# Sparse attention and soft mixture of experts on one core: the factor on the keys moves from the key tile to the instruction that negates the scores

## The chip, the cores and the metric

One Trainium2 chip, one of its cores. The metric is the device time of one execution in microseconds (us); the kernel before was run three times: 547.24, 548.01 and 548.21 us, median 548.01 us. The engines are called PE (TensorE; PEld is its weight load), DVE (VectorE), ACT (ScalarE), POOL (GpSimd) and SP (SyncE, which here issues the DMAs).

## The reference

Attention over 8 batches and 8 heads, 576 tokens, head size 64, in fp32. Scores that lie more than `tau` below their row's maximum are dropped, and the output of attention feeds a soft mixture of experts (8 experts with 4 slots each, hidden size 1024).

```
scores = scale * q @ k.T                     # scale = 1/8
thresh = max(scores, -1) - tau
scores = where(scores >= thresh, scores, -1e9)
attn   = exp(scores - max(scores, -1));  attn /= sum(attn, -1) + 1e-9
x      = (attn @ v), heads side by side      # 4608 x 512
logits = x @ phi                             # 4608 x 32
slots  = softmax(logits, over tokens).T @ x; out_e = relu(slots_e @ w1_e) @ w2_e
out    = softmax(logits, over slots) @ out_e
```

## The kernel before, in words

The 64 heads are worked on as 32 pairs (two heads of a batch, one on the upper and one on the lower 64 partitions), four pairs to a batch. For a pair SP loads the keys into a tile `k` (128 x 576, L525), the queries into `q` (L530) and the values into `vv` (L537); `k` and `q` have two buffers each.

Before the keys are used they are multiplied by `flag8`, a column of 128 numbers that holds 1/8 (or 0 for a negative tau; L392): for the first pair by two instructions of DVE, one per half of the tile (128 x 288), for the other 31 pairs by one instruction of POOL on the whole tile (both L532).

A pair then has nine blocks of scores. For each block
- PE computes q times k into one of four PSUM regions `ps` (L552, for the ninth block L557),
- DVE reads the region once and writes the negated scores `ss` to SBUF, and on the way takes their minimum, the negated maximum, as the column `nmx` (L564; the profile names it TENSOR_SCALAR_CACHE_REDUCE, with a DVE_READ_ACCUMULATOR behind it). Here it is called the negation,
- ACT computes the exponential into `p` (L574),
- POOL adds |tau| to the column `nmx`, which gives `thr` (L577),
- DVE compares `ss` with `thr`, multiplies `p` by the result and sums the rows (L580, SCALAR_TENSOR_TENSOR). Here it is called the masking.

PE transposes `p` (L478), ACT copies the transposes out of PSUM (L483), and PE multiplies them with the values (L670). POOL and DVE form reciprocals of the row sums (L604, L607, L615, L618), which POOL applies (L611, L689). At the end of a batch come the logits (L752) and the sums of the slots (L800, L805, L813). Behind the last pair the experts' weights (`w`, `host`) are used and the output is written (L997 to L1086).

The order of all instructions up to the last pair is computed when the kernel is built: class `Order` holds each step with its engine, a duration, its dependences and a due time (`TABLE`, by the number of the step in its scope). A planner then goes through time, and gives each engine that is free the step with the earliest due time whose inputs are there and which has room in its buffers. `G.skip(n)` counts numbers without adding a step, so that the due times of the steps behind keep their places. Each engine carries out its list in this order and waits on semaphores; `qload` holds the number of the step that loads the queries of a pair, behind which two weight loads are put.

Of the kernel before, what the change touches and what calls it, by code (L numbers as in the profile page):

```python
# [10 lines left out]
F32 = mybir.dt.float32  # L11
F32R = mybir.dt.float32r
AF = mybir.ActivationFunctionType
ALU = mybir.AluOpType
# [8 lines left out]
    k=2, q=2, vv=2, r=3, ri=3, nmx=4, thr=4, p2=4, pL=1, pTa=1, pTb=1, pTl=1, l4=1,  # L23
    ss=4, xT=5, x=1, xl=1, dT=1, d=1, M=2, f=2,
# [313 lines left out]
def softmax_attention_soft_moe(  # L338
# [17 lines left out]
    nc = tc.nc  # L356
# [9 lines left out]
    HS = S // 2  # L366
# [3 lines left out]
    cp = ctx.enter_context(tc.tile_pool(name="consts", bufs=1))  # L370
# [8 lines left out]
        out=st1, in_=ident.rearrange("p (g s) -> p s g", g=4), axis=AX.X, op=ALU.add  # L379
# [8 lines left out]
    phi_sb = cp.tile([128, HP, NS], F32, name="phi_sb")  # L388
    tau_sb = cp.tile([128, 1], F32, name="tau_sb")
    nc.sync.dma_start(tau_sb, tau.to_broadcast([128, 1]))  # L390
    flag8 = cp.tile([128, 1], F32, name="flag8")
    nc.vector.tensor_scalar(  # L392
        out=flag8, in0=tau_sb, scalar1=0.0, scalar2=0.125, op0=ALU.is_ge, op1=ALU.mult
    )
    NR = 4 * B + B // 2
    lall = cp.tile([128, NR, NS], F32, name="lall")
# [18 lines left out]
    with tc.tile_pool(name="ps_up", bufs=1, space=PSUM) as up:  # L415
# [6 lines left out]
        k=([128, S], F32), q=([128, 2, S], F32), vv=([128, 640], F32), r=([128, N9], F32), ri=([128, N9], F32),  # L422
        nmx=([128, 1], F32), thr=([128, 1], F32), p2=([128, 2 * S], F32), pL=([128, S], F32),
        pTa=([128, 2, 4, QA], F32), pTb=([128, 2, 4, S - QA], F32), pTl=([128, S], F32), l4=([128, 192], F32),
        ss=([128, S], F32), xT=([128, S], F32), x=([128, 4, DM], F32), xl=([128, DM], F32), dT=([128, 192], F32),
# [5 lines left out]
    G = Order(kinds)  # L431
# [14 lines left out]
    n = NPRE + NHOST  # L446
# [44 lines left out]
    def dve(dur, nom, r, w, fn):  # L491
        G.add("DVE", dur, nom, fn, r, w)
# [11 lines left out]
    def pair(p):  # L504
        b, j = divmod(p, HP)
        t0 = p * N9
        late = p == NP - 1
        G.scope("first" if p == 0 else "last" if p == NP - 1 else f"pair{j}", t0)
        kt, qt, vv = (Buf(k) for k in ("k", "q", "vv"))
# [5 lines left out]
        def pool(dur, nom, fn, r, w):  # L515
            G.add("POOL", dur, nom, fn, r, w)


        one = dict(scalar2=1.0, op0=ALU.mult, op1=ALU.mult)
        parts = [(h,) for h in range(2)] if p == 0 else [(0, 1)]  # L520
        for hs in parts:
            kc, n = slice(hs[0] * HS, (hs[-1] + 1) * HS), len(hs)
            def keys(a=hs[0], z=hs[-1] + 1):
                for g in range(2):
                    nc.sync.dma_start(  # L525
                        kt.t[rows[g]].rearrange("p (h k) -> p h k", h=2)[:, a:z],
                        kT[b, j, :, 0:2 * S].rearrange("d (h g k) -> d g h k", h=2, g=2)[:, g, a:z])
            G.add("SP", 1340 if p else 700, t0 - 18 + hs[0], keys, w=[kt[h] for h in hs])
            for g in range(2):
                G.add("SP", (625 if p == 0 else 1250) if p < 3 else 800, t0 - 18 + hs[0], lambda g=g, a=hs[0], z=hs[-1] + 1: nc.sync.dma_start(  # L530
                    qt.t[rows[g], a:z], qT[b, j, :, a:z]), w=[qt[h, g] for h in hs])
            sc = lambda e, kc=kc: lambda: e.tensor_scalar(out=kt.t[:, kc], in0=kt.t[:, kc], scalar1=flag8, **one)  # L532
            if p == 0:
                G.add("DVE", 370, t0 - 9 + hs[0], sc(nc.vector), [], [kt[h] for h in hs])
            else:
                pool(730, t0 - 9, sc(nc.gpsimd), [], [kt[h] for h in hs])
        G.add("SP", 1400 if p < 3 else 800, t0 - 12, lambda: nc.sync.dma_start(vv.t, vt[b, j]), w=[vv], after=vload[-1:])  # L537
        vload.append(len(G.ops) - 1)
        qload.append(len(G.ops) - 2 - (p > 0))

# [1 line left out]
        for i in range(N9):  # L544
            t = t0 + i
            s, nmx, thr = Buf("s"), Buf("nmx"), Buf("thr")
            c, h = divmod(i, 2)

            def qk(i=i, c=c, h=h, s=s):
# [12 lines left out]
            ss = Buf("ss")  # L562

            dve(674, t + OFF['mx'], [s], [ss, nmx], lambda s=s, ss=ss, nmx=nmx: nc.vector.tensor_scalar(  # L564
                out=ss.t.rearrange("p (a k) -> p a k", a=2), in0=s.t[:, :, 0:HS], scalar1=-1.0, scalar2=3.4028234663852886e38,
                op0=ALU.mult, op1=ALU.min, accum_out=nmx.t))
            sv = lambda ss=ss: ss.t.rearrange("p (a k) -> p a k", a=2)
            if i == 8:
# [1 line left out]
            else:  # L570
                if h == 0:
# [6 lines left out]
                out=thr.t, in0=nmx.t, scalar1=1.0, scalar2=pabs, op0=ALU.mult, op1=ALU.add), [nmx], [thr])  # L578
            G.add("DVE", 738, t + OFF['st'], port=True, r=[ss, thr], w=[dst, r[i]],
                fn=lambda sv=sv, thr=thr, view=view, i=i: nc.vector.scalar_tensor_tensor(  # L580
                    out=view().rearrange("p (a k) -> p a k", a=2), in0=sv(),
                    scalar=thr.t, in1=view().rearrange("p (a k) -> p a k", a=2),
                    op0=ALU.is_le, op1=ALU.mult, accum_out=r.t[:, i:i + 1]))

            if late and i == 8:
                dve(70, t + OFF['ri'], [r], [ri], lambda: nc.vector.tensor_scalar(
                    out=ri.t, in0=r.t, scalar1=1e-9, scalar2=None, op0=ALU.add))
# [14 lines left out]
            elif i == 8:  # L602
                e = slice(i // 2 * 2, i + 1)
                pool(292, t + OFF['ri'], lambda e=e: nc.gpsimd.tensor_scalar(  # L604
                    out=ri.t[:, e], in0=r.t[:, e], scalar1=1e-9, scalar2=1.0, op0=ALU.add, op1=ALU.mult),
                    [r[k] for k in range(e.start, e.stop)], [ri[c]])
                dve(84, t + OFF['ri'], [], [ri[c]], lambda e=e: nc.vector.reciprocal(ri.t[:, e], ri.t[:, e]))  # L607
                for k in range(e.start, e.stop):
# [3 lines left out]
                        out=view(), in0=view(), scalar1=ri.t[:, k:k + 1], **one), [ri[c]], [dst_])  # L612
            elif not late and h == 1:
                if i == 7:
                    pool(292, t + OFF['ri'], lambda: nc.gpsimd.tensor_scalar(  # L615
                        out=ri.t[:, 0:8], in0=r.t[:, 0:8], scalar1=1e-9, scalar2=1.0, op0=ALU.add, op1=ALU.mult),
# [43 lines left out]
        for a, (pT, q) in enumerate(((pTa, slice(0, QA)), (pTb, slice(QA, S)))):  # L660
            n0 = u + OFF['a1' if a else 'a0']
            w = bank_of(p == NP - 1)
            n = q.stop - q.start
# [10 lines left out]
            if late:  # L674
                dve(69 + 1.04 * n, n0 + OFF['ae'], [w, spreads[0]], [xT[a]], lambda w=w, q=q, n=n: nc.vector.tensor_tensor(
                    out=xT.t[:, q], in0=lone(w)[:, 0:n], in1=spreads[0].t[:, q], op=ALU.mult))
# [9 lines left out]
        if not late:  # L686
# [3 lines left out]
                out=wide(), in0=wide(), in1=ri.t[:, 0:8].rearrange("p (c h) -> p c h", h=2).unsqueeze(3).to_broadcast(  # L690
                    [128, 4, 2, 64]), op=ALU.mult))
# [159 lines left out]
    recent, last, vload, qload = [], [], [], []  # L851
    for p in range(NP):
        recent.append(len(G.ops))
        pair(p)
        if p % HP == HP - 1:
            dispatch(p // HP)
# [54 lines left out]
    for i in range(NHOST):  # L911
        n = next(n for n in reversed(range(len(cells))) if sum(map(bytes_of, cells[n:])) >= (i + 1) * 4096)
# [262 lines left out]
```

## Time and profile before

| what | value |
|---|---|
| runs | 547.24, 548.01, 548.21 us; median 548.01 us |
| span of the profiled execution (first to last instruction) | 546.2 us |
| median of the runs less this span | 1.8 us |
| PE, PEld busy | 527.5 us (97%), 337.0 us (62%) |
| DVE, ACT, POOL busy | 471.0 us (86%), 457.4 us (84%), 242.1 us (44%) |
| mean granted clock of TensorE | 0.993 of full speed |

The page gives no other time for the profiled execution than its span; the 1.8 us are taken for what lies around it. Busy time is the union of an engine's instructions. A DVE instruction's row ends some 0.07 us after the start of the next one, so how long an instruction holds DVE is read from one start to the next. Ends of matmuls are modelled, so that a PE row may hide a short wait. Under "idle before" stands the idle time of the engine ahead of an instruction, and what ended it.

### The profile page before, as it was taken

The page shows a single profiled execution, that of the slowest core. Times are in us where ns is not written, and L with a number is a line of the kernel's source. Part 1 is how long each engine was busy: PE and PEld are TensorE (multiplying, and loading weights), DVE is VectorE, ACT ScalarE, POOL GpSimd, SP SyncE. Part 2 cuts the span into 40 slices and gives each one's busy share as a digit, 9 for nine tenths or more (in the row PEclk, how much of TensorE's full clock was granted, in tenths as well). Part 3 has the DMA queues.
Part 4 walks back from the last instruction along what each step waited for, and adds up shares of the span by engine and source line. Part 5 has one row for each costly group of instructions (what it writes and reads, how often), then busy time and mean ns, then how long its engine had stood idle before and what let it go on. Part 6 is the DMA issues. An engine that isn't in the chain of part 4 may idle for free.

```text
span 546.2 us, 18324 instructions
## 1 busy us (share of the span) xinstructions
PE 527.5 (97%) x7029; PEld 337.0 (62%) x7029; DVE 471.0 (86%) x1332; ACT 457.4 (84%) x790; POOL 242.1 (44%) x475
## 2 busy tenths in 40 slices
PE   8999999999999999999999999999999999999990
PEld 6666666666666666666666666666666656644470
DVE  5999998999999999999899989999999999523192
ACT  3899998999899989999999989999999888621181
POOL 2554555554545464545355545545454524121030
PEclk9999999999999999999999999999999999999997
DMA  6355555565535543333333333333333322999498
GB/s 176 74 158 178 168 167 169 138 190 161 166 90 167 172 153 122 92 94 86 78 91 92 91 91 92 91 91 91 91 90 91 91 76 69 336 410 408 197 375 316
DMA packets 31990, 83.03 MB, mean 152 GB/s; under 512 B 4640, under 2 KB 12832, under 8 KB 31904
## 3 DMA queue, kind: packets, MB, share of 16 engines
q1 hardware_dynamic: 31904, 81.87, 48.8%
q8 instruction: 55, 0.90, 0.7%
q14 instruction: 31, 0.25, 0.2%
HBM read 72.42 MB, written 9.44 MB: 150 GB/s over the span
## 4 chain that ended last, share of the span: by engine, by line
PE 82%; DVE 5%; DMA 5%; ACT 4%; issue 2%; DVEq 0%; POOL 0%; SPq 0%; POOLq 0%; ACTq 0%
PE ps L670 29%; PE ps L552 24%; PE ps L478 17%; DMA w<-in_w 5%; PE ps L557 3%; PE ps L694 2%; PE ps L752 2%; PE ps L800 1%; DVE p L580 1%; PE up L418 1%; DVE cT L989 1%; DVE host L1086 1%; ACT pTa L483 1%; DVE ss L564 1%; PE ps L470 1%
## 5 line engine op out<-in xcount | busy, mean ns | idle before, releaser
L564 DVE TENSOR_SCALAR_CACHE_REDUCE ss<-ps 128x576 f32<-128x576 f32 x288 | 209.1, 752 | 15.5 <-ACT pTl L483 4.8
L577 POOL TENSOR_SCALAR thr<-nmx,pabs 128x1 f32<-128x1 f32 x288 | 132.2, 461 | 187.0 <-DVE ss L564 167.7
L580 DVE SCALAR_TENSOR_TENSOR p<-ss,thr,p 128x576 f32<-128x576 f32 x256 | 201.8, 823 | 3.4 <-ACT p L574 3.1
L574 ACT ACTIVATE p<-ss,nmx 128x576 f32<-128x576 f32 x256 | 188.2, 781 | 18.3 <-DVE ss L564 18.2
L552 PE MATMUL ps<-k,q 64*128 64x288 f32 x1024 | 167.2, 427 | 1.0 <-ACT pTb L483 0.4
L478 PE MATMUL ps<-ident,p 64*128 64x64 f32 x2304 | 98.2, 223 | 0.9 <-ACT pTa L483 0.3
L478 PEld LDWEIGHTS ps<-ident,p 64*128 64x128 f32 x2304 | 87.8, 138 | 17.8 <-issue 3.3
L552 PEld LDWEIGHTS ps<-k,q 64*128 64x128 f32 x1024 | 83.3, 188 | 21.9 <-ACT pTl L652 5.8
L483 ACT COPY pTb<-ps 128x1024 f32<-128x1024 f32 (+1 forms) x96 | 84.0, 876 | 5.7 <-PE ps L478 3.5
L670 PE MATMUL ps<-pTb,vv 128*64 128x320 f32 x512 | 76.0, 439 | 0.4 <-DVE pTl L652 0.4
L483 ACT COPY pTa<-ps 128x1024 f32<-128x1024 f32 x64 | 64.9, 1018 | 0.4 <-PE ps L478 0.4
L670 PE MATMUL ps<-pTa,vv 128*64 128x256 f32 x512 | 62.3, 385 | 0.0
L670 PEld LDWEIGHTS ps<-pTb,vv 128*64 128x64 f32 x512 | 34.1, 136 | 36.4 <-issue 9.0
L670 PEld LDWEIGHTS ps<-pTa,vv 128*64 128x64 f32 x512 | 33.9, 136 | 26.2 <-DVE ss L564 8.5
L670 PE MATMUL ps<-pTl,vv 128*64 128x256 f32 (+1 forms) x256 | 41.9, 406 | 0.0
L689 POOL TENSOR_TENSOR x<-x,ri 128x512 f32<-128x512 f32 x31 | 32.3, 1043 | 4.8 <-ACT x L483 4.8
L483 ACT COPY xT<-ps 128x256 f32<-128x256 f32 (+1 forms) x62 | 24.6, 398 | 6.2 <-PE ps L670 5.2
L670 PEld LDWEIGHTS ps<-pTl,vv 128*64 128x64 f32 x256 | 18.5, 137 | 12.6
L580 DVE SCALAR_TENSOR_TENSOR pL<-ss,thr,pL 128x576 f32<-128x576 f32 x32 | 26.0, 812 | 0.0
L574 ACT ACTIVATE pL<-ss,nmx 128x576 f32<-128x576 f32 x32 | 24.8, 776 | 0.4 <-DVE ss L564 0.4
L954 POOL TENSOR_TENSOR c<-lall,crow 128x512 f32<-128x512 f32 x9 | 9.3, 1046 | 35.7 <-PE ct L470 21.4
L483 ACT COPY pTl<-ps 128x256 f32<-128x256 f32 x64 | 24.2, 378 | 0.4 <-PE ps L478 0.4
(165 smaller groups left out, 550.3 us busy)
## 6 DMA issues: line engine op xcount, KB each, us to landing
w<-in_w SPq DMA_DIRECT2D x44, 512.0 KB, 7.3
q<-in_qT SPq DMA_DIRECT2D x62, 288.0 KB, 4.5
vv<-in_vt SPq DMA_DIRECT2D x32, 320.0 KB, 4.6
host<-in_w SPq DMA_DIRECT2D x20, 512.0 KB, 7.8
k<-in_kT SPq DMA_DIRECT2D x62, 144.0 KB, 3.0
out<-w SPq DMA_DIRECT2D x8, 512.0 KB, 3.4
out<-host SPq DMA_DIRECT2D x8, 512.0 KB, 5.0
out<-host SPq DMA_DIRECT2D x4, 256.0 KB, 4.6
```

What stands on the lines that cost most here:

```text
L478: nc.tensor.transpose(out=s[:, g, c:c + 64], in_=ins[g], identity=ident[rows[g], rows[g]], tile_position=(64 * g, 0))
L483: G.add("ACT", 51 + 0.833 * n, nom, lambda: nc.scalar.copy(*io()), r, w)
L552: nc.tensor.matmul(s.t[:, g, 0:HS], qt.t[rows[g], h, c * 128:(c + 1) * 128], kt.t[rows[g], h * HS:(h + 1) * HS], start=True, stop=True, ti ...
L557: nc.tensor.matmul(s.t[rows[a], g, 0:HS], qt.t[rows[g], a, SM:S], kt.t[rows[g], a * HS:(a + 1) * HS], start=True, stop=True, tile_position ...
L564: dve(674, t + OFF['mx'], [s], [ss, nmx], lambda s=s, ss=ss, nmx=nmx: nc.vector.tensor_scalar(out=ss.t.rearrange("p (a k) -> p a k", a=2), ...
L574: G.add("ACT", 668, t + OFF['ex'], lambda sv=sv, nmx=nmx, view=view: nc.scalar.activation(view().rearrange("p (a k) -> p a k", a=2), sv(), ...
L577: pool(250, t + OFF['th'], lambda nmx=nmx, thr=thr: nc.gpsimd.tensor_scalar(out=thr.t, in0=nmx.t, scalar1=1.0, scalar2=pabs, op0=ALU.mult, ...
L580: fn=lambda sv=sv, thr=thr, view=view, i=i: nc.vector.scalar_tensor_tensor(out=view().rearrange("p (a k) -> p a k", a=2), in0=sv(), scalar ...
L670: nc.tensor.matmul(lone(w)[h * 64:(h + 1) * 64, 0:n], vv.t[:, v0:v0 + 64], p0, start=(kb == 0), stop=(kb == 4), tile_position=(0, h * 64), ...
L689: G.add("POOL", 1040, u + 6.8, own=f"new{j}", r=[ri[0]], w=[x[j]], fn=lambda: nc.gpsimd.tensor_tensor(out=wide(), in0=wide(), in1=ri.t[:, ...
L694: nc.tensor.transpose(out=w.t[:, g, c * 64:c * 64 + 64], in_=xj()[rows[g], c], identity=ident[rows[g], rows[g]], tile_position=(64 * g, 0))
L752: nc.tensor.matmul(lone(wl)[c * 32:(c + 1) * 32, o], phi_sb[:, k, :], xT[k].t[:, q(c)], start=(k == 0 and not o.start), stop=(k == HP - 1) ...
```

## The change

The column becomes `nflag8` = -1/8 (or 0), and the negation multiplies by that column where it multiplied by the constant -1.0. The two instructions of DVE and the 31 of POOL on the keys are left out. `G.skip(1)` stands in their place, and the number in `qload` is corrected for the step that is no longer there.

```
-    flag8 = cp.tile([128, 1], F32, name="flag8")
+    nflag8 = cp.tile([128, 1], F32, name="nflag8")
     nc.vector.tensor_scalar(
-        out=flag8, in0=tau_sb, scalar1=0.0, scalar2=0.125, op0=ALU.is_ge, op1=ALU.mult
+        out=nflag8, in0=tau_sb, scalar1=0.0, scalar2=-0.125, op0=ALU.is_ge, op1=ALU.mult
     )
...
-            sc = lambda e, kc=kc: lambda: e.tensor_scalar(out=kt.t[:, kc], in0=kt.t[:, kc], scalar1=flag8, **one)
-            if p == 0:
-                G.add("DVE", 370, t0 - 9 + hs[0], sc(nc.vector), [], [kt[h] for h in hs])
-            else:
-                pool(730, t0 - 9, sc(nc.gpsimd), [], [kt[h] for h in hs])
+            G.skip(1)
...
-        qload.append(len(G.ops) - 2 - (p > 0))
+        qload.append(len(G.ops) - 2)
...
             dve(674, t + OFF['mx'], [s], [ss, nmx], lambda s=s, ss=ss, nmx=nmx: nc.vector.tensor_scalar(
-                out=ss.t.rearrange("p (a k) -> p a k", a=2), in0=s.t[:, :, 0:HS], scalar1=-1.0, scalar2=3.4028234663852886e38,
+                out=ss.t.rearrange("p (a k) -> p a k", a=2), in0=s.t[:, :, 0:HS], scalar1=nflag8, scalar2=3.4028234663852886e38,
                 op0=ALU.mult, op1=ALU.min, accum_out=nmx.t))
```

The changed file is five lines shorter from the keys on, so that the negation is L564 before and L559 after, the scores L552 and L547, the masking L580 and L575.

On DVE at the start of the kernel (first the columns made from tau, then the first blocks of pair 0) the order before is:

```order
L392 TENSOR_SCALAR flag_78<-tau_sb 128x1
L407 TENSOR_SCALAR nabs<-tau_sb 128x1
L409 TENSOR_SCALAR pabs<-nabs 128x1
L532 TENSOR_SCALAR k_312<-k_312,flag_78 128x288 x2
L378 TENSOR_REDUCE st_66<-ident 128x32
L564 TENSOR_SCALAR ss_216,nmx_268<-ps_336 128x576
L564 TENSOR_SCALAR ss_240,nmx_256<-ps_337 128x576
```

The same place with the change:

```order
L392 TENSOR_SCALAR nflag_78<-tau_sb 128x1
L407 TENSOR_SCALAR nabs<-tau_sb 128x1
L409 TENSOR_SCALAR pabs<-nabs 128x1
L378 TENSOR_REDUCE st_66<-ident 128x32
L559 TENSOR_SCALAR ss_216,nmx_268<-ps_336,nflag_78 128x576
L559 TENSOR_SCALAR ss_240,nmx_256<-ps_337,nflag_78 128x576
```

The two instructions on `k` are gone, and the negation has the column as one more input. The rest of DVE's list stands in the same order to its end.

On POOL in the second pair (`thr` is the threshold, `ri` the reciprocals, `pL` the ninth block) the order before is:

```order
L615 TENSOR_SCALAR ri_280<-r_308 128x8
L577 TENSOR_SCALAR thr_292<-nmx_300,pabs 128x1
L532 TENSOR_SCALAR k_312<-k_312,flag_78 128x576
L577 TENSOR_SCALAR thr_248<-nmx_268,pabs 128x1
L577 TENSOR_SCALAR thr_260<-nmx_256,pabs 128x1
```

With the change:

```order
L610 TENSOR_SCALAR ri_280<-r_308 128x8
L572 TENSOR_SCALAR thr_292<-nmx_300,pabs 128x1
L572 TENSOR_SCALAR thr_248<-nmx_268,pabs 128x1
L572 TENSOR_SCALAR thr_260<-nmx_256,pabs 128x1
```

One instruction of 128 x 576 per pair is gone from between the thresholds, and nothing else is moved. PE, ACT and SP have the same instructions in the same order as before; of the PSUM regions two change their places at a few steps.

## Rows read from the trace of the kernel before

**Rows 1.** The page: busy time of the engines, and the clock granted to TensorE in 40 slices.

```profile
PE 527.5 (97%) x7029; PEld 337.0 (62%) x7029; DVE 471.0 (86%) x1332; ACT 457.4 (84%) x790; POOL 242.1 (44%) x475
PEclk9999999999999999999999999999999999999997
```

**Rows 2.** Busy time in four stretches: the first pairs, the middle, the last pairs, the experts. Columns: us, then PE, PEld, DVE, ACT, POOL busy (instructions), granted clock, DMA share, GB/s.

```profile
20.00:47.80 27.80, 27.00 (x328) 16.71 (x326) 27.18 (x78) 25.07 (x42) 15.42 (x29) 1.00 0.53 142
47.80:434.00 386.20, 386.00 (x5440) 250.90 (x5438) 367.75 (x1056) 365.07 (x627) 195.23 (x378) 1.00 0.42 118
434.00:470.00 36.00, 35.12 (x532) 22.49 (x529) 32.62 (x89) 32.79 (x58) 13.67 (x27) 1.00 0.39 114
470.00:546.20 76.20, 61.37 (x591) 33.25 (x588) 28.96 (x68) 24.07 (x51) 10.91 (x26) 0.95 0.89 347
```

**Rows 3.** The chain of work that ended last: by engine over the whole span, by line between 20 and 47.8 us, and one of its pieces in the last pairs (start, us, what).

```profile
PE 82%; DVE 5%; DMA 5%; ACT 4%; issue 2%; DVEq 0%; POOL 0%; SPq 0%; POOLq 0%; ACTq 0%
...
by line: PE ps L552 17.5%; PE ps L670 16.6%; DVE ss L564 13.8%; DVE p L580 11.0%; issue 10.4%; ACT pTa L483 10.3%; PE ps L478 10.3%; ACT pL L574 4.8%; ACT p L574 2.5%; ACT xT L483 1.8%; PE ps L694 0.9%; DVE ri L618 0.4%; DVE ri L607 0.3%; D
...
441.65 0.50 DVE ss L564
```

**Rows 4.** Groups of instructions by form. Columns: line, engine, operation, out<-in, count, busy us, mean ns of one, idle us before them and what ended it.

```profile
L564 DVE TENSOR_SCALAR_CACHE_REDUCE ss<-ps 128x576 f32<-128x576 f32 x288 | 209.1, 752 | 15.5 <-ACT pTl L483 4.8 <-PE ps L552 4.2 <-ACT pTa L483 1.9
L532 POOL TENSOR_SCALAR k<-k,flag 128x576 f32<-128x576 f32 x31 | 24.2, 780 | 0.7 <-DMA k<-in_kT 0.3
```

**Rows 5.** Line 532, the factor on the keys: durations in ns (least/median/most), first and last start in us, and who waited for it (no row follows: nobody).

```profile
L532 POOL TENSOR_SCALAR k<-k,flag x31: 737/743/1240, 11.7 to 436.5; 128x576 f32<-128x576 f32 x31
L532 DVE TENSOR_SCALAR k<-k,flag x2: 370/370/371, 4.2 to 6.8; 128x288 f32<-128x288 f32 x2
...
who waited for it (us, times):
```

**Rows 6.** The first scores, all engines in order of time (start, us, engine, line, operation).

```profile
6.38 0.44 PE L470 MATMUL ps<-ident 128*128 128x128 f32 x2
6.75 1.03 PEld L552 LDWEIGHTS ps<-k,q 64*128 64x128 f32 x10 [0.17 <-issue]
...
6.82 0.37 DVE L532 TENSOR_SCALAR k<-k,flag 128x288 f32<-128x288 f32 x1 [2.24 <-DMA k<-in_kT]
...
7.10 0.37 DVE L378 TENSOR_REDUCE st<-ident 128x32 f32<-128x128 f32 x1
7.58 0.76 DVE L564 TENSOR_SCALAR_CACHE_REDUCE ss<-ps 128x576 f32<-128x576 f32 x1
```

**Rows 7.** Instructions of DVE with and without a column as an operand. L409 has constants alone, L407 has the column `tau_sb`, all on 128 x 1; L813 has the column `f`, L1058 has none, both with one tensor in PSUM and one in SBUF. Columns as in rows 4, or start and us.

```profile
3.39 0.20 DVE L407 TENSOR_SCALAR nabs<-tau_sb 128x1 f32<-128x1 f32 x1
3.63 0.15 DVE L409 TENSOR_SCALAR pabs<-nabs 128x1 f32<-128x1 f32 x1
...
L813 DVE SCALAR_TENSOR_TENSOR acc<-acc,f,ps 128x256 f32<-128x256 f32 x2 | 1.0, 476 | 0.0
...
L1058 DVE TENSOR_TENSOR so_sb<-h00e,so_sb 128x256 f32<-128x256 f32 x1 | 0.4, 425 | 9.4 <-issue 9.4
```

**Rows 8.** DVE through one pair in the middle of the kernel, from the pause behind one reciprocal (L607) to the next, in order of time; left out are most of the instructions between, which follow with pauses of some hundredths of a microsecond or none, and two of 0.1 to 0.2 us.

```profile
277.41 0.15 DVE L607 RECIPROCAL ri<-ri 128x1 f32<-128x1 f32 x1
277.97 0.76 DVE L564 TENSOR_SCALAR_CACHE_REDUCE ss<-ps 128x576 f32<-128x576 f32 x1 [0.41 <-ACT pTl L483]
...
279.40 0.75 DVE L564 TENSOR_SCALAR_CACHE_REDUCE ss<-ps 128x576 f32<-128x576 f32 x1
...
280.08 0.75 DVE L564 TENSOR_SCALAR_CACHE_REDUCE ss<-ps 128x576 f32<-128x576 f32 x1
...
280.76 0.81 DVE L580 SCALAR_TENSOR_TENSOR p<-ss,thr,p 128x576 f32<-128x576 f32 x1
...
281.50 0.81 DVE L580 SCALAR_TENSOR_TENSOR p<-ss,thr,p 128x576 f32<-128x576 f32 x1
...
290.98 0.15 DVE L607 RECIPROCAL ri<-ri 128x1 f32<-128x1 f32 x1
291.53 0.76 DVE L564 TENSOR_SCALAR_CACHE_REDUCE ss<-ps 128x576 f32<-128x576 f32 x1 [0.39 <-ACT pTl L483]
```

**Rows 9.** A place at which PE needs the PSUM region that DVE has just read: DVE's instructions ahead of it in order of time, and PE's next weight load into that region.

```profile
248.46 0.76 DVE L564 TENSOR_SCALAR_CACHE_REDUCE ss<-ps 128x576 f32<-128x576 f32 x1
...
254.14 0.76 DVE L564 TENSOR_SCALAR_CACHE_REDUCE ss<-ps 128x576 f32<-128x576 f32 x1
254.83 0.08 DVE L564 DVE_READ_ACCUMULATOR ss<-ps 128x1 f32 x1
...
254.96 0.42 PEld L552 LDWEIGHTS ps<-k,q 64*128 64x128 f32 x4
```

**Rows 10.** The masking beside POOL's work on the keys: its durations over the kernel (ns, least/median/most), and two places in order of time.

```profile
L580 DVE SCALAR_TENSOR_TENSOR p<-ss,thr,p x256: 710/812/1327, 10.4 to 468.1; 128x576 f32<-128x576 f32 x128
...
205.29 0.74 POOL L532 TENSOR_SCALAR k<-k,flag 128x576 f32<-128x576 f32 x1
...
205.70 0.93 DVE L580 SCALAR_TENSOR_TENSOR p<-ss,thr,p 128x576 f32<-128x576 f32 x1
...
436.48 0.74 POOL L532 TENSOR_SCALAR k<-k,flag 128x576 f32<-128x576 f32 x1
...
436.50 1.33 DVE L580 SCALAR_TENSOR_TENSOR p<-ss,thr,p 128x576 f32<-128x576 f32 x1
```

More of the change, by code (lines that the diff above doesn't have):

```diff
@@ L521, in pair @@
         for hs in parts:
-            kc, n = slice(hs[0] * HS, (hs[-1] + 1) * HS), len(hs)
             def keys(a=hs[0], z=hs[-1] + 1):
```

## The prediction

> **What bounds the kernel now.** I read the page's busy times first. PE is busy for 97% of the span, DVE for 86%, ACT for 84%, POOL for 44%, and TensorE has its full clock in all slices but the last [rows 1]. The table by stretches comes next: from 47.8 to 434 us PE is busy for 386.0 of 386.2 us, DVE for 367.8 and ACT for 365.1 [rows 2]. So PE sets the pace there, with two engines 5% below it and POOL at half. Before 47.8 us DVE is nearly full too (27.2 of 27.8 us) and PE has some idle time, and the last stretch is one of DMAs, which starts when attention gives its buffers free. Then the chain: 82% PE, 5% DVE, no POOL over the span, but 13.8% negation and 11.0% masking between 20 and 47.8 us [rows 3]. What the reader is to see: an engine that has 5% to spare is not free to grow, because its pauses are small and PE, DVE and ACT wait for each other block by block.
>
> **What goes: POOL's part.** 31 instructions of 780 ns, 24.2 us of POOL [rows 4]. Nobody waits for them [rows 5], and POOL isn't on the chain [rows 3]. The keys of a pair are then ready as soon as they have landed, but they were ready early before. Worth 0 on the path by POOL's own time.
>
> **What goes: DVE's part.** Two instructions of 370 ns at the start [rows 5]. The second runs from 6.82 us, and the reduction behind it ends at 7.47, while PE loads the first queries only at 6.75, behind transposes that wait for nothing of DVE; the first negation at 7.58 waits for PE's scores [rows 6]. So PE is late there, not DVE: 0 to 0.1 us, I take 0.
>
> **What comes: a column as an operand, 288 times.** The negation reads one tensor from PSUM with constants alone and takes 752 ns [rows 4]; from one start to the next it holds DVE for 0.68 us (279.40 to 280.08), the masking for 0.74 us (280.76 to 281.50) [rows 8]. No row shows a negation with a column, so I bound it. From below: 0, since a further operand gives the instruction nothing to leave out. From above: the 0.06 us by which the masking, which has a column and a second tensor, holds DVE longer. Between them lie two pairs of rows: on 128 x 1 the same operation takes 0.20 us with a column and 0.15 without, and on 256 elements from PSUM and SBUF 476 ns with and 425 without [rows 7]. Both give 50 ns, and the first is the same operation, so I take 50 ns: 288 x 0.05 = 14.4 us more work on DVE.
>
> [...]
>
> **How much of the 14.4 us reaches the end.** A pair takes (470 - 7.6) / 32 = 14.45 us [rows 2, 6] and has nine negations, so DVE gets 0.45 us more per pair. In the middle it has 386.2 - 367.8 = 18.4 us of idle time [rows 2], over 26.7 pairs 0.69 us per pair. The added work fits, so DVE doesn't become the bound as a whole. But it comes late within each pair: between two pauses the lateness grows by 50 ns per negation, and the pause of 0.4 us behind L607 (277.97, 291.53) takes it back [rows 8]. What counts is who needs DVE's result in between with less margin than that.
> - *Middle.* At 248.46 us five negations begin, up to that at 254.14, with no pause of DVE between; it gives its PSUM region free at about 254.90, and PE loads weights for that region at 254.96 [rows 9]. There is no margin, and five times 50 ns make 0.25 us. This place comes once in a batch of four pairs. Others in the batch have a lateness of 0.05 to 0.25 us and a margin of 0.05 to 0.2; I put them together at 0.1 us (an estimate from the same kind of reading; its ends are 0 and 0.45 per pair). 26.7 / 4 = 6.7 batches of 0.35 us: 2.3 us.
> - *First pairs.* Between 20 and 47.8 us the chain spends 13.8% of 27.8 us, 3.8 us, in negations of 0.68 us each [rows 3, 8], which is five or six, and the pauses of DVE add up to 0.6 us [rows 2]. Some 19 negations lie there (27.8 / 14.45 x 9 = 17, and the first pairs are denser). On the chain 6 x 0.05 = 0.3; all of them less the pauses 19 x 0.05 - 0.6 = 0.35; before 20 us DVE works nearly without pause too. I take 0.5 us.
> - *Last pairs.* From 434 to 470 us PE is idle for 0.9 us and the chain goes through DVE again [rows 2, 3]: six to nine negations on it or ahead of it, 0.3 us.
> - *Experts.* They have no negation. They start later by what attention ends later, and their weights with them: 0.
>
> Given back: a masking that meets POOL's work on the keys takes 0.93 us in place of 0.81 (205.29 and 205.70), once 1.33 (436.48 and 436.50) [rows 10]. Only these long ones profit. If this happens in one pair of each batch, it is 7 x 0.12 + 0.5 = 1.3 us of DVE; the places have pauses behind them, so I count 0.1 us on the path.
>
> **Sum.** 2.3 + 0.5 + 0.3 - 0.1 = +3.0 us. The profiled span of 546.2 becomes 549.2 us; with the 1.8 us that lie between it and the median of the runs, 551.0 us.
>
> **Rivals.**
> 1. *DVE becomes the bound.* If a negation grows by more than 0.69 / 9 = 77 ns, or if the lateness of one pair is still there when the next begins, PE waits for DVE in every pair. For it speaks that PE, DVE and ACT are coupled without margin [rows 9]; against it, that the nearest rows give 50 ns and the highest bound 60. With half of the 14.4 us on the path it is +7 us (555), with all of it +14.4 (562).
> 2. *The pauses take it.* PE's records are modelled, and a weight load that is late by 0.1 to 0.2 us may still be hidden by the matmuls in front of it. Then the middle costs nothing and the first and last pairs 0.5 us: 548.5 us, no change that can be told. What speaks for it is that DVE has 0.69 us per pair and needs 0.45.
> 3. *Faster.* POOL's work on the keys held up the maskings, and the column is free. Then 1.3 us of DVE come back [rows 10], mostly where the chain goes through DVE, with 0.1 us at the start, and nothing is paid: 546.7 us. It decides if the negation stays at 752 ns. For it: the long maskings stand right beside L532. Against it: rows 7, and that most maskings take the median of 812 ns. [...]
>
> That the change doesn't do what it says is no rival: the order shows the 33 instructions gone and the column on every negation.
>
> **How the numbers follow.** Forecast (a part reaches the end, 549.2 to 555): 0.53. Rival 1 (above 555): 0.11. Rival 2: 0.25. Rival 3: 0.11. A measurement of this kernel tells 0.2% from no change, 1.1 us here (546.9 to 549.1). So slower 0.53 + 0.11 = 0.64, same 0.25, faster 0.11. The likeliest is 551.0 us; its own range is 549.2 to 555. The range for 8 in 10 goes down into rival 2 and just into rival 3, to 547.1, and up into rival 1, to 557: 0.05 to 0.1 are left out on either side.
>
> **What would show it.** The negation's mean at about 800 ns, with 0.73 us from start to start, and DVE busy for some 483 us (471 - 0.7 - 1.3 + 14.4); if it stays at 752, the step on the column is wrong and rival 3 is on. POOL at 218 us, with no line for the keys, and no masking of 0.93 us in the middle. The middle of 386.2 us grown by about 2.3 us, with PE's weight loads behind a negation later by up to 0.25 us; if it has grown by 7 us or more, rival 1; if by less than 0.5, rival 2. The start of the first negation still at about 7.6 us. The forecast is wrong if the granted clock of the middle isn't full any more, which nothing here speaks for.

## The result, and the profile after

The changed kernel takes 553.46 us (median of four runs, 552.77 to 553.74), the kernel before beside it 548.11 us (four runs, 547.24 to 548.91): ratio 1.0093, 95% interval 1.0080 to 1.0107. It is slower by 5.35 us, where +3.0 us was forecast. The profiled execution has a span of 551.0 us against 546.2. One execution of run 5 below, of 556.88 us, fell in a slower state with a granted clock of 0.941, and the figures given for that run leave it out.

The page's busy times, with the clock in 40 slices, answer to [rows 1]:

```profile
PE 529.8 (96%) x7029; PEld 336.6 (61%) x7029; DVE 480.7 (87%) x1330; ACT 458.7 (83%) x790; POOL 214.9 (39%) x444
PEclk9999999999999999999999999999999999999996
```

DVE is busy for 9.7 us more and POOL for 27.2 us less; PE and ACT have the same instructions as before, and their busy times are 2.3 and 1.3 us longer. The clock is full up to the last slice, as before. The middle, in the columns of [rows 2]:

```profile
47.80:434.00 386.20, 384.99 (x5383) 248.64 (x5384) 372.79 (x1046) 363.50 (x624) 169.53 (x348) 1.00 0.42 118
```

In the same 386.2 us PE got through 57 instructions fewer (5383 for 5440), while its busy time fell by only 1.0 us: short waits of PE are partly inside its modelled durations, so the busy share doesn't show the loss and the starts of the instructions must be compared. The groups of the negation, the masking and the exponential, in the columns of [rows 4]:

```profile
L559 DVE TENSOR_SCALAR_CACHE_REDUCE ss<-ps,nflag 128x576 f32<-128x576 f32 x288 | 224.0, 810 | 12.8 <-PE ps L547 7.0 <-ACT pTa L483 1.7 <-issue 1.6
L575 DVE SCALAR_TENSOR_TENSOR p<-ss,thr,p 128x576 f32<-128x576 f32 x256 | 198.9, 812 | 3.9 <-ACT p L569 3.7
L569 ACT ACTIVATE p<-ss,nmx 128x576 f32<-128x576 f32 x256 | 188.6, 777 | 22.3 <-DVE ss L559 21.8
```

A negation with the column takes 810 ns for 752, 58 ns more. Who waited for the negation (us, times), first in the kernel before, then in the changed one. POOL, ACT and PE's weight loads for the products with the values (L670, then L665) and for the scores (L552, then L547) all wait longer in total:

```profile
  POOL thr L577: 167.7, 159
  ACT p L574: 18.2, 19
  PEld ps L670: 8.5, 21
...
  PEld ps L552: 0.6, 2
```

```profile
  POOL thr L572: 199.9, 206
  ACT p L569: 21.8, 21
  PEld ps L665: 13.6, 34
  PEld ps L547: 5.9, 18
```

The place of [rows 9], in the changed kernel: DVE's instructions in order of time, then PE's two weight loads for scores.

```profile
251.72 0.77 DVE L559 TENSOR_SCALAR_CACHE_REDUCE ss<-ps,nflag 128x576 f32<-128x576 f32 x1
252.41 0.81 DVE L559 TENSOR_SCALAR_CACHE_REDUCE ss<-ps,nflag 128x576 f32<-128x576 f32 x1
...
257.58 0.08 DVE L575 DVE_READ_ACCUMULATOR p<-ss,thr,p 128x1 f32 x1
257.58 0.81 DVE L559 TENSOR_SCALAR_CACHE_REDUCE ss<-ps,nflag 128x576 f32<-128x576 f32 x1
258.32 0.08 DVE L559 DVE_READ_ACCUMULATOR ss<-ps,nflag 128x1 f32 x1
```

```profile
257.80 0.30 PEld L547 LDWEIGHTS ps<-k,q 64*128 64x128 f32 x4 [0.44 <-ACT pTb L483]
258.46 0.30 PEld L547 LDWEIGHTS ps<-k,q 64*128 64x128 f32 x4 [0.35 <-DVE ss L559]
```

Before, the load at 254.96 has no idle time ahead of it [rows 9]; now PE's loader is held up for 0.35 us until the negation that began at 257.58 has read its region. This is the wait that the prediction described.

To see where the time went I matched PE's steps one by one (their order is the same in both kernels) and took the difference of their start times. Apart from the start of the kernel it grows in three ways: by 0.3 to 0.4 us in each batch at the same few places behind negations; by about 0.2 us at each of five places, one in a batch from 152 us on, where the long product of `x` (L800 before, L795 now) begins; and in the first pairs. At the end of attention it is 5.15 us, and the experts are shifted along.

### The profile page after: what moved, and what is told of

The parts are those of the page before. It is cut to its first block, busy times and chain, and to the rows that moved or that the text cites. A ratio compares the mean times of both kernels' runs of the same rounds, so it can differ in the third digit from the quotient of the medians.

```text
span 551.0 us, 18253 instructions
## 1 busy us (share of the span) xinstructions
PE 529.8 (96%) x7029; PEld 336.6 (61%) x7029; DVE 480.7 (87%) x1330; ACT 458.7 (83%) x790; POOL 214.9 (39%) x444
## 4 chain that ended last, share of the span: by engine, by line
PE 76%; ACT 11%; DVE 5%; issue 2%; DVEq 0%; ACTq 0%
PE ps L665 26%; PE ps L547 21%; PE ps L478 15%; PE ps L552 3%; PE h L992 3%; ACT p L569 3%; PE so L1027 2%; ACT pTa L483 2%; PE ps L689 2%; PE ps L795 1%; ACT pTb L483 1%; ACT xT L483 1%; DVE cT L984 1%; DVE host L1081 1%; ACT xT L692 1%
## 5 line engine op out<-in xcount | busy, mean ns | idle before, releaser
L559 DVE TENSOR_SCALAR_CACHE_REDUCE ss<-ps,nflag 128x576 f32<-128x576 f32 x288 | 224.0, 810 | 12.8 <-PE ps L547 7.0
L575 DVE SCALAR_TENSOR_TENSOR p<-ss,thr,p 128x576 f32<-128x576 f32 x256 | 198.9, 812 | 3.9 <-ACT p L569 3.7
L547 PE MATMUL ps<-k,q 64*128 64x288 f32 x1024 | 169.2, 429 | 2.5 <-DVE ss L559 1.5
L547 PEld LDWEIGHTS ps<-k,q 64*128 64x128 f32 x1024 | 83.4, 188 | 25.2 <-DVE ss L559 5.9
L665 PE MATMUL ps<-pTb,vv 128*64 128x320 f32 x512 | 76.0, 439 | 0.2 <-DVE pTl L647 0.2
L665 PE MATMUL ps<-pTa,vv 128*64 128x256 f32 x512 | 62.3, 385 | 0.0
L665 PEld LDWEIGHTS ps<-pTb,vv 128*64 128x64 f32 x512 | 34.1, 136 | 36.3 <-DVE ss L559 5.0
L665 PEld LDWEIGHTS ps<-pTa,vv 128*64 128x64 f32 x512 | 33.9, 136 | 26.3 <-DVE ss L559 8.5
L665 PE MATMUL ps<-pTl,vv 128*64 128x256 f32 (+1 forms) x256 | 41.9, 406 | 0.0
L665 PEld LDWEIGHTS ps<-pTl,vv 128*64 128x64 f32 x256 | 18.4, 137 | 12.6
L575 DVE SCALAR_TENSOR_TENSOR pL<-ss,thr,pL 128x576 f32<-128x576 f32 x32 | 26.0, 811 | 0.0
L606 POOL TENSOR_SCALAR pL<-pL,ri 128x576 f32<-128x576 f32 x31 | 22.9, 739 | 2.3 <-issue 0.3
```

The source lines that it names most:

```text
L547: nc.tensor.matmul(s.t[:, g, 0:HS], qt.t[rows[g], h, c * 128:(c + 1) * 128], kt.t[rows[g], h * HS:(h + 1) * HS], start=True, stop=True, ti ...
L606: pool(725, t + OFF['sc'], lambda k=k, view=view_: nc.gpsimd.tensor_scalar(out=view(), in0=view(), scalar1=ri.t[:, k:k + 1], **one), [ri[c ...
L665: nc.tensor.matmul(lone(w)[h * 64:(h + 1) * 64, 0:n], vv.t[:, v0:v0 + 64], p0, start=(kb == 0), stop=(kb == 4), tile_position=(0, h * 64), ...
```

## The experiments

Theory at the outset: the column's 58 ns on 288 negations are the loss, in the middle and in the first and last pairs, and the factor on the keys was worth nothing. Rivals: the keys' instructions being gone does harm of its own; or the order, which stayed as it was, no longer fits. Each kernel was timed beside the kernel before in five rounds; the median of before was 547.81 us in the first four runs, 548.10 in the second four, 548.34 in the third three and 548.49 in the last.

**1. The constant alone.** From the changed kernel:

```
-    ... scalar1=nflag8, scalar2=3.4028234663852886e38,
+    ... scalar1=-0.125, scalar2=3.4028234663852886e38,
```

> The changed kernel with the constant -0.125 in the negation in place of the column; the factor 0 for a negative tau is left out. Theory A (the column is the whole loss, and leaving the factor on the keys out is worth nothing): 548.1 us, ratio to the kernel before 0.9985 to 1.0015, negation back at 752 ns. Rival B (a part of the loss comes from elsewhere, as PE now waiting for the keys' DMA itself): 549.5 to 551 us, ratio 1.003 to 1.006. Rival C (leaving the factor on the keys out gives time back, and the column costs more than the loss): below 547.3 us, ratio under 0.9985.

Measured: 549.25 us (548.61 to 550.58), ratio 1.0026, interval 1.0017 to 1.0035. That lies between what A and B give, and some 1.4 us of the loss have nothing to do with the column.

**2. The column alone.** From the kernel before, with its keys still scaled:

```
+    minus = cp.tile([128, 1], F32, name="minus")
+    nc.vector.memset(minus, -1.0)
...
-    ... scalar1=-1.0, scalar2=3.4028234663852886e38,
+    ... scalar1=minus, scalar2=3.4028234663852886e38,
```

> The kernel before, keys scaled as before, with a column of -1 in the negation in place of the constant -1.0. Theory A: the whole loss, 552.9 to 553.9 us, ratio 1.008 to 1.0105, negation at 810 ns. Rival B: a part of it, 550 to 552 us, ratio 1.004 to 1.007. Rival C: more than the loss, 554.3 us or more, ratio 1.0115 and up, since the work on the keys is still there.

Measured: 551.37 us (550.66 to 552.13), ratio 1.0062, interval 1.0050 to 1.0074: +3.6 us from the column by itself. So two causes add up.

**3 and 4. The column in the middle pairs, and in the first and last pairs.** From the changed kernel, `p` being the number of the pair:

```
+    ... scalar1=nflag8 if 3 <= p < 30 else -0.125, ...     # column_middle
+    ... scalar1=-0.125 if 3 <= p < 30 else nflag8, ...     # column_ends
```

> The changed kernel with the column in pairs 3 to 29 alone, and the constant -0.125 in the other five pairs (there the factor 0 for a negative tau is left out). By the drift of PE between the two traces (about 0.53 us per batch of four pairs, 6.7 batches) theory A says +3.6 us, 551.4 to 552.0, ratio 1.006 to 1.007. The prediction's own term was +2.3 (550.4, 1.004). Rival (DVE is late in the middle only because the first pairs made it late): +1 us or less, ratio under 1.002.

> The reverse: the column in pairs 0 to 2, 30 and 31 alone, the constant -0.125 in pairs 3 to 29. Theory A: +1.0 to +1.6 us (549.1 to 549.7, ratio 1.002 to 1.003), so that middle and ends add up to the whole. The prediction's terms were 0.5 and 0.3: +0.8 (548.9, 1.0015). Rival (the pieces don't add up, the loss in the middle rests on the ends): +3 us or more, ratio over 1.005.

Measured: 552.12 us (ratio 1.0079, 1.0064 to 1.0094) and 550.85 us (1.0050, 1.0038 to 1.0062); their traces have 243 and 45 negations with the column, as meant. Above the constant alone the middle costs 2.9 us and the five pairs at the ends 1.6 us; together 4.5, the 4.2 us by which the changed kernel lies above it within the spread. PE's starts, from one execution of each kernel, give 2.4 and 1.1 us from 10 us to the end of attention, and 3.4 with the column everywhere: the two parts add up. Of the 1.1 us at the ends 0.95 have arisen by 47 us, and 0.2 arise in the last pairs.

**What the 1.4 us are.** With the constant alone, PE's starts against before jump by 0.2 us at the five places (151.8, 209.6, 267.3, 324.9, 382.5 us) and elsewhere only the first 10 us (0.2 us, less than runs 1 and 9, one and the same kernel, differ by there) and the experts (0.25 us) leave a difference that lasts. All orders are the same; what differs there are two PSUM regions. The text on the change speaks of two regions at a few steps; the planner's own lists show three. Regions 0 and 2 also change their places at steps of the first pairs, until 49 us, but from 11 us to 77 us PE's starts lie later by a constant 0.20 us, so that swap costs nothing. The order of PE with its numbers at the second of the places, before and changed:

```
L800 MATMUL ps_336<-x_152,d_160 32x512 x4        L795 MATMUL ps_335<-x_152,d_160 32x512 x4
L805 MATMUL ps_336<-xl_156,d_160 32x128 x4       L800 MATMUL ps_335<-xl_156,d_160 32x128 x4
L800 MATMUL ps_335<-ones,d_160 32x1 x4           L795 MATMUL ps_336<-ones,d_160 32x1 x4
```

The long product takes the region that the short one had. By the code the planner gives out the lowest-numbered region that is empty at the time of its plan, and with the keys' step out of the plan that is the other one. In the chip's time it isn't empty: ACT is still copying out of it. First the kernel before at this place (ACT's copy, then PE's weight loads), then the kernel with the constant:

```profile
209.25 0.59 ACT L483 COPY pTb<-ps 128x512 f32<-128x512 f32 x1
...
209.62 0.16 PEld L800 LDWEIGHTS ps<-x,d 128*32 128x32 f32 x8 [0.39 <-ACT d L483]
```

```profile
209.69 0.59 ACT L483 COPY pTb<-ps 128x512 f32<-128x512 f32 x1
...
210.28 0.19 PEld L795 LDWEIGHTS ps<-x,d 128*32 128x32 f32 x8 [0.61 <-ACT pTb L483]
```

Before, the load began 0.37 us after the start of the copy and before its end; now it begins at its end, 0.59 us after. The 0.22 us between could be read from the trace of before: the copy's end at 209.84 less the load at 209.62. Three runs test this against rivals.

**5. The constant with the old regions.** From the kernel before; the planner still counts a step for the keys, which issues nothing:

```
-            sc = lambda e, kc=kc: lambda: e.tensor_scalar(out=kt.t[:, kc], in0=kt.t[:, kc], scalar1=flag8, **one)
+            sc = lambda e: lambda: None
...
-    ... scalar1=-1.0, ...
+    ... scalar1=-0.125, ...
```

> The constant -0.125 in every negation and no instruction on the keys, as in the run that left the keys' factor out alone and took 549.25 us; but here the planner still counts a step of the old length for the keys, which issues nothing, so that it gives out the PSUM regions as in the kernel before. (The factor 0 for a negative tau is left out.) The trace of the earlier run against before shows PE later by 0.20 to 0.22 us at five places, one per batch from 151.8 us on, where the long product of the probabilities with x got ps0 in place of ps1 and waits for ACT's copy out of ps0. Theory A, the regions are the cost: without the swap 5 x 0.20 = 1.0 us come back, 548.2 us, within 0.1% of before. Rival B, the keys' instructions being gone costs by itself (POOL runs ahead, PE meets the keys' DMA): still 549.2 us. Rival C: swaps in the first pairs cost too, and all of the 1.4 us come back: 547.8 us.

Measured: 548.34 us (547.17 to 549.20), ratio 1.0001, interval 0.9991 to 1.0011. Theory A. By PE's starts this kernel ends attention 0.03 us from before: the keys' instructions were worth nothing, and neither does their absence cost anything.

**6. The changed kernel with the old regions.** As 5, with `scalar1=nflag8`:

> The changed kernel with the column, but with the empty step for the keys in the plan, so that the PSUM regions are given out as in the kernel before. Theory A (five places of 0.20 us, and they add to what the column costs): 553.4 - 1.0 = 552.4 us, ratio 1.008 to before. Rival B (the regions cost nothing): 553.4 us, 1.010. Rival C (regions of the first pairs too): 552.0 us, 1.0075. Rival D: the late negations of the column hide the wait for ps0, so the swap costs nothing beside the column: 553.4 us although the run with the constant gains.

Measured: 552.06 us (551.51 to 553.59), ratio 1.0074, 1.0061 to 1.0087: 1.4 us below the changed kernel, and 3.7 above run 5, which is the column. The time is C's 552.0, and A's 552.4 is inside the interval too. PE's starts speak for A: the changed kernel is later than this one by 0.81 us at 10 us and by 1.81 at the end of attention, 1.0 us in between. D is out: swap and column add up.

**7. The kernel before with the five swaps.**

```
+        x = None
+        for i in sorted(range(len(start)), key=lambda i: (start[i], i)):
+            if self.ops[i][0] == "PE":
+                y = next((q for q in self.ops[i][4] if q.kind == "s"), None)
+                if x and slot[x][0] == 1 and slot[y][0] == 0 and self.ops[i][1] == 200:
+                    slot[x], slot[y] = slot[y], slot[x]
+                x = y if self.ops[i][1] == 1000 else None
```

> The kernel before, with its keys scaled and its constant -1.0, and one thing changed: at the five places (one per batch, 151.8 to 382.5 us) the product of the probabilities with x takes ps0 and the short one behind it ps1, as in the changed kernel. Theory A: 5 x 0.20 = +1.0 us, 548.8 us, PE idle for 0.18 us ahead of the long product for ACT's copy at each place. Rival B: 547.8 us, as before.

Measured: 549.28 us (548.65 to 549.72), ratio 1.0018, 1.0009 to 1.0026, +1.2 us with not one instruction changed. For PE's instructions that read `x`, what ended PE's idle time ahead of them (us, times), first in the kernel before, then with the swaps:

```profile
  ACT pTb L483: 0.2, 1
```

```profile
  ACT pTb L490: 1.1, 6
```

Five waits more of 0.18 us each, 0.9 us: theory A.

**8. The sign on ACT.** The constant -0.125 in the negation, and a column of -1 or 0 as the scale of ACT's exponential (the column for the threshold is then made by one short instruction at the start in place of two):

```
-    ... AF.Exp, bias=nmx.t, scale=-1.0)
+    ... AF.Exp, bias=nmx.t, scale=nflag)
```

> Another way to take the factor from the keys: VectorE's negation uses the constant -0.125, and the sign of tau comes in as a column (-1 or 0) that ACT's exp takes as its scale in place of the constant -1; the threshold's column is made huge for a negative tau, with one short instruction less at the start. Regions as in the changed kernel. If a column as scale costs ACT nothing (the exp has a column as bias already): 549.2 us, as the run with the constant alone. If it costs ACT some 0.05 us as it did VectorE, 288 x 0.05 = 14.4 us more on ACT, which has pauses of 21 us in the middle: 550 to 553 us. It keeps the same results as the reference, so it is also the version that would beat the changed kernel by 4 us.

Measured: 561.20 us (560.15 to 562.09), ratio 1.0237, 1.0221 to 1.0252: above the range, and no version that beats anything. The exponential's row:

```profile
L567 ACT ACTIVATE p<-ss,nmx,nflag 128x576 f32<-128x576 f32 x256 | 211.8, 872 | 16.6 <-DVE ss L557 16.1
```

In run 1 the same row, and the middle in the columns of [rows 2], were:

```profile
L569 ACT ACTIVATE p<-ss,nmx 128x576 f32<-128x576 f32 x256 | 188.4, 780 | 18.4 <-DVE ss L559 18.4
```

```profile
47.80:434.00 386.20, 385.10 (x5410) 250.48 (x5408) 365.64 (x1052) 364.20 (x624) 172.83 (x349) 1.00 0.42 118
```

So ACT pays 92 ns for the column, 26 us in all, on an engine whose idle time in the middle was 22.0 us (386.2 - 364.2).

**9. Half of the columns, a miss.** The edit was meant to use the column in odd blocks only:

```
+    ... scalar1=nflag8 if i % 2 else -0.125, ...
```

> The changed kernel with the column in the odd blocks alone (four of a pair's nine negations), the constant -0.125 in the five others; regions as in the changed kernel, so this starts from the 549.25 us of the run with the constant alone, and the column in all blocks adds 4.2 us to that. (For a negative tau the factor 0 is left out in five blocks.) Theory A, lateness adds up over the negations between two pauses and reaches PE in proportion: 4/9 x 4.2 = 1.9 us, 551.1 us. Rival B, small lateness is hidden by what margin there is and only a full run of late negations reaches PE: 549.8 us or less.

Measured: 548.96 us (548.47 to 550.34), ratio 1.0019. The group in its trace says what ran:

```profile
L559 DVE TENSOR_SCALAR_CACHE_REDUCE ss<-ps 128x576 f32<-128x576 f32 x288 | 209.1, 752 | 19.5 <-PE ps L547 7.8 <-ACT pTl L483 5.3 <-ACT pTa L483 1.9
```

All 288 negations have constants alone: the function is called after the loop, when `i` is 8. It is a second run of the constant alone (549.25 in run 1) and says nothing on its question. The names in a group's row show such a slip at once.

**10. Two columns.** The cap of the minimum as a second column:

```
+    top = cp.tile([128, 1], F32, name="top")
+    nc.vector.memset(top, 3.4028234663852886e38)
...
+    ... scalar1=nflag8, scalar2=top, ...
```

> The changed kernel, with its second constant (3.4e38, the cap of the minimum) a column too. Does a second column cost again, and does VectorE become the bound beyond the 77 ns that the prediction worked out from its pauses? Theory A, every column costs 0.058 us: the negation at 0.87 us, VectorE short of time by (116 - 77) x 9 x 26.7 pairs = 9 us in the middle, on top of what 77 ns cost in proportion (4.2 x 77 / 58 = 5.6 us from 549.25): 564 us, VectorE busy for over 98% of the middle. Rival B, in proportion still: 549.25 + 2 x 4.2 = 557.7 us. Rival C, the second column is read beside the first and costs nothing: 553.5 us with the negation still at 0.81 us.

Measured: 563.12 us (562.45 to 563.45), ratio 1.0268, 1.0251 to 1.0285. The negation and the middle:

```profile
L561 DVE TENSOR_SCALAR_CACHE_REDUCE ss<-ps,nflag,top 128x576 f32<-128x576 f32 x288 | 240.8, 869 | 7.5 <-PE ps L549 4.3 <-ACT pTa L485 1.4
```

```profile
47.80:434.00 386.20, 381.80 (x5268) 241.74 (x5268) 377.88 (x1022) 358.52 (x611) 166.53 (x339) 1.00 0.41 117
```

Each column costs 58 to 59 ns, DVE is busy for 97.8% of the middle, a little under the 98% expected, and the time is theory A's, 564. The second column costs 9.7 us where the first costs 4.2: from a pace limited by PE to one limited by DVE.

**11. The planner told.** One duration, a negation counts 732 and not 674:

```
-            dve(674, t + OFF['mx'], [s], [ss, nmx], ...
+            dve(732, t + OFF['mx'], [s], [ss, nmx], ...
```

> The changed kernel with one number of the planner changed: a negation counts 732 in place of 674, by the 58 that the column adds. The order of the work and the regions may then come out otherwise on all engines. Theory A, the order made for the longer negation puts PE's work so that less of it waits: 551 to 553 us. Rival B, the table of start times was found for the old durations, and a planner that moves work against it loses as much or more: 553.5 us or above.

Measured: 606.16 us (604.76 to 608.37), ratio 1.1064, 1.1041 to 1.1086. B, and far beyond it: the order is another on every engine. The chain by engine:

```profile
PE 37%; ACT 23%; DVE 13%; issue 5%; DVEq 0%; ACTq 0%
```

The negation takes 810 ns as in the changed kernel, but PE has only 37% of the chain (82% before, [rows 3]). The table of due times and the durations belong together; which of its steps moves first these rows do not show.

**12. Half of the columns.** As 9, with the block's number bound when the function is made (`i=i` in its arguments):

> What the kernel of the run before, column_half, was to be: the column in the odd blocks alone (four of a pair's nine negations), the constant -0.125 in the others. (The trace of column_half shows all 288 negations with constants alone, since its block number was read after the loop had ended, so it was a second run of the kernel with the constant: 548.96 us beside 549.25.) Regions as in the changed kernel. (For a negative tau the factor 0 is left out in five blocks.) Theory A, lateness adds up over the negations between two pauses and reaches PE in proportion: PE's weight load at the place of the five negations in a row (about 257 us) later by two or three times 58 ns, 0.12 to 0.17 us, in place of 0.29, and the time 549.1 + 4/9 x 4.3 = 551.0 us. Rival B, margins of the size of 0.1 us take the small lateness, and what two columns cost above one (9.7 us above 4.3) goes on downward: 549.8 us or less, with no step at most of the places where the changed kernel has one.

Measured: 550.00 us (549.25 to 550.98), ratio 1.0031, 1.0021 to 1.0040. Its negations:

```profile
L559 DVE TENSOR_SCALAR_CACHE_REDUCE ss<-ps 128x576 f32<-128x576 f32 x160 | 118.6, 752 | 9.6 <-PE ps L547 4.3 <-ACT pTl L483 2.1 <-ACT pTa L483 1.7
L559 DVE TENSOR_SCALAR_CACHE_REDUCE ss<-ps,nflag 128x576 f32<-128x576 f32 x128 | 102.0, 810 | 6.6 <-PE ps L547 3.7 <-issue 1.9 <-ACT pTl L483 0.3
```

The time lies between the two expectations, nearer to B. PE's starts show why both are half right. Against run 9, the load of the five negations is late by 0.17 us, three times 58 ns: in proportion, as A says. PE's next step takes 0.16 us of it back, nearly all. With the column everywhere (run 6 against run 5) the same load is late by 0.29 us and 0.23 of it comes back. So the lateness is proportional, and it looks as if there were a margin of some 0.23 us behind the place; that margin is read off these two cases and was not tried by itself. A few steps on, 0.05 us are left with the odd blocks and 0.17 with all. At the end of attention 4/9 of the columns make PE 0.96 us late, not the 1.9 of the first expectation, nor the 1.5 that 4/9 of the 3.4 us between runs 5 and 6 would be.

## Why the prediction was right, and which steps were off

The sign, the mechanism and the range were right; the size was 2.4 us short. By the prediction's own terms:

- **The keys: 0 for POOL's part, 0 for DVE's part.** Right. Run 5 takes both away with everything else kept: 1.0001. The 0.1 us counted as given back isn't in it, and the third rival's faster kernel isn't either. DVE does get back the 1.3 us that were estimated: in run 5 the maskings of 0.93 us and the one of 1.33 [rows 10] are gone. But six of 1.04 to 1.05 us stay, one in most batches, beside POOL's product on `x` and not beside the keys (run 5):

```profile
140.10 1.04 POOL L689 TENSOR_TENSOR x<-x,ri 128x512 f32<-128x512 f32 x1 [0.23 <-ACT x L483]
...
140.71 1.04 DVE L580 SCALAR_TENSOR_TENSOR p<-ss,thr,p 128x576 f32<-128x576 f32 x1
```

  Here the masking starts 0.43 us before the end of the product. With the column the maskings come later: in the changed kernel seven start 0.03 to 0.04 us before the end of that product (from 85.14 to 434.54 us) and take 0.81 to 0.82 us, the longest of all takes 910 ns (1327 before), and POOL is busy for 214.9 us (forecast 218). What in the two instructions makes the masking longer, no run shows.
- **The column: 50 ns.** Measured 58, just inside the bound of 60 that the masking gave. From start to start it is 0.74 us (7.73 to 8.47 in the changed kernel) for a forecast of 0.73. The first pair of [rows 7] was no clean comparison, since L407 has not only a column but also a second operation that L409 lacks. L392, with two operations and constants alone, takes 0.15 us like L409, so the 50 ns there are the column's:

```profile
3.32 0.15 DVE L392 TENSOR_SCALAR flag<-tau_sb 128x1 f32<-128x1 f32 x1 [1.70 <-DMA tau_sb<-in_tau]
```

  The other pair differs by an operation too, and no row settles it. With 58 for 50 the +3.0 becomes 3.5, which is the difference of the spans of run 6 and before (549.7 and 546.2); in part this is luck, since the middle would then be 2.7 us for a measured 2.4 and the first pairs 0.6 for 0.7 or more. DVE's 480.7 us for a forecast of 483 is luck too: the column adds 16.7 us and not 14.4, the maskings give back 2.8 (from 823 to 812 ns on average) and not 1.3, and DVE's rows lie over each other for 3.6 us more, with fewer pauses between them. With no, one and two columns the negation takes 752, 810 and 869 ns (run 9, the changed kernel, run 10): 58 and 59 ns for each, against the 50 of [rows 7].
- **Middle, 2.3 us.** Right in size. Between runs 5 and 6 PE's starts drift apart from 0.74 us at 60 us to 3.13 at 430, 2.4 us, 0.35 us for a batch. But the split in a batch was off: the place of [rows 9], put at 0.25, keeps 0.17 (0.29 late, 0.23 taken back, 0.11 lost again two steps on), and the others, put at 0.1, keep 0.18.
- **First pairs, 0.5 us.** Too small: 0.7 by 47 us between runs 5 and 6, 0.95 between runs 1 and 4. **Last pairs, 0.3 us:** 0.2.
- **The step that failed is one that the sum doesn't have.** The text on the change says that two PSUM regions change their places at a few steps, and the prediction gave this no term: in effect 0 us. It costs 0.9 us by the waits of run 7, 1.2 by its time and 1.4 by run 6 against the changed kernel (1.0 by PE's starts there). That the result still fell into the range owes nothing to this term: run 6, without it, lies in the range as well (552.06). The prediction looked at the orders, which were the same, and at who needs DVE; who needs ACT's copies earlier it didn't ask.
- **First negation still at about 7.6 us.** It came at 6.99 in the profiled execution, since PE's first transposes took 1.76 us for 2.56. They take between 1.63 and 2.56 in the profiles of these kernels, and in runs 1 and 9, one and the same kernel, PE's step behind them began at 5.71 and 6.30, so this isn't the change's. What they won was lost again at once: the second lot of scores waits 1.25 us. The row names a negation, but DVE reads the region that is needed by 7.73; what came late in this execution was a transfer of queries. It landed at 9.46 us (8.70 before), 0.09 us ahead of this lot of scores in either kernel (9.55 and 8.79). The times from issue to landing (least/median/most, of `q` up to 12 us, first before, then changed):

```profile
DMA to landing us min/median/max: 2.9/3.0/5.7
```

```profile
DMA to landing us min/median/max: 2.7/3.4/6.8
```

  PE's second lot of scores begins between 8.7 and 9.6 us in these profiles. Part of the 5.15 us by which this one execution is late lies there (some 0.7 us). In runs 1 and 9, the same kernel, it begins at 9.00 and 8.70, so 0.3 us of such a difference come by chance; whether all of it does was not tried.
- **Rival 1** had its threshold at 77 ns: one column (58) stays below it, two (117) go above, with the time worked out from it (564 for 563.12). The 0.69 us of idle time per pair was the right thing to read. **Rival 2** holds in part: run 12 shows PE's margins taking most of a small lateness, but not the 0.29 us of the whole change.

Taken together: column 3.7 us (run 6 less run 5), regions 1.2 us (run 7), keys 0: 4.9 us of 5.35, inside the interval of 4.4 to 5.9. The rest isn't assigned.

No kernel here beats the one before. Run 6 is the better form of the change (552.06), and the change without its column is as fast as before (548.34), but has no place for the factor 0 of a negative tau.

## What to carry to other kernels

When instructions that nobody waits for are taken out of a kernel whose order and buffers come from a planner, compare the buffers as well as the order: a swapped region is a changed dependence, and its price can be estimated from the old trace as the end of the last reader of the other region less the start of the new user (here 0.22 us, for 0.18 us of waiting measured). A swap is not always paid for: the one in the first pairs cost nothing (run 1, PE later by a constant 0.20 us from 11 to 77 us). An operand that turned from a constant into a column was added work on every instruction here (58 ns on DVE's negation, 92 on ACT's exponential), and the 24.2 us taken from POOL were worth nothing (run 5, ratio 1.0001): it is worth removing work from an idle engine only if the busy one pays nothing for it. Lateness between two pauses added up in proportion (0.17 us for three negations with the column, 0.29 for five), but what reaches the end did not: 4/9 of the columns cost less than 4/9 of the time, and two columns cost 13.9 us above the constant alone where one costs 4.2.

## What the runs showed of the hardware that was not expected

- A column of 128 numbers in place of a constant costs DVE 58 ns on a negation of 128 x 576 (752 to 810 ns), a second one another 59 (869). On ACT a column as the exponential's scale costs 92 ns (780 to 872), though the instruction has a column as its bias already.
- PE's records hide short waits: in the middle its busy time is 1.0 us less, but 57 instructions fewer are done, which at 71 ns each (386.0 us for 5440) would be 4.0 us.
- Maskings that run beside POOL's product on `x` take 1.04 to 1.05 us for 0.81 in run 5, which has no instruction on the keys; the one shown starts 0.43 us before the product's end. In the changed kernel, where they start 0.03 to 0.04 us before its end, they take 0.81 to 0.82.
